# A new order for the first slots of a fused attention and MLP kernel, and a reordered end of batch 6

## Chip, cores and metric

The kernel runs on one core of a Trainium2 chip. The metric is the device time of one execution in microseconds (us); lower is better. TensorE (PE) does the matrix products, VectorE (DVE), ScalarE (ACT) and GpSimd (POOL) the elementwise work, and SyncE (SP) issues most DMAs.

## What is computed

```
def _attn_ref(x, state):                       # x: 8 batches, 8 heads, 512 x 64; state: 8, 8, 32 x 64
    a  = softmax(scale * x @ state.T);   xread = a  @ state
    a2 = softmax(scale * state @ x.T);   sread = a2 @ x
    return concatenate([xread, sread], axis=2)
def _moe_ref(x, w_in, w_out):                  # x: 4608 x 512 (heads side by side), w_in 512 x 2048
    h = x @ w_in
    g = h * tanh(softplus(h))
    return g @ w_out                           # w_out 2048 x 512
```

All of it is float32. The kernel splits every operand of a large product into a high part (a cast to a shorter float) and a low part (a subtraction), and adds three products: high by high, high by low, low by high. The weights arrive as 64-bit words and are made into floats on the chip: a scaling of the upper words (`hi`, `ho`; on DVE's help `ki`, `ko`), a rounding of the lower words (`ci`, `co` on ACT, `di`, `do` on DVE) and a join of both by DVE (`ji`, `jo`).

## The kernel before, in words

A batch goes through 16 chunks of the inner dimension of 2048, two to a slot, so eight slots. For the attention's read of x the kernel never forms xread: it multiplies the state's blocks with a slice of w_in once per slot (`sw_slice`, L576, tile `swp` in PSUM, cast to `swh` by ACT, low part `swl` by DVE), and then multiplies the softmax weights (`ah`, `al`, L469) with that (`gemm1`, L628, tile `ph`). ACT applies the activation (`mish`), a cast and a subtraction give `gh` and `gl`, and these are multiplied with w_out (`gemm2`, L700, tiles `acc`, for batch 0; `consume`, L1011, with seven products of sums, for later batches). The matrix `swp` comes from products on quarters of the PE array, which take few columns each.

**Order.** Nothing is ordered by a planner. Each of PE, DVE, ACT and POOL runs its instructions in exactly the order in which the program issues them (`InOrder`, L60). For batch 0 a long string of steps (L874 to L886) writes that order out by hand: each word names a step of the dictionary `steps` (L830), and a step that is a generator does one part at each mention. The names that matter: `sw0` (product, then ACT's cast, then DVE's low part of slice 0), `no` (softmax sums and normalizing), `pr0`, `pr1` (transpose on PE, `ah` by ACT, `al` by DVE of either half of the tokens), `fill` (matmuls on data at hand whose result is not used, two records for each), `qa`, `qb` (`first_quarter`, L761: slot 0's `gemm1` for one half of the tokens, for chunk a or b), `p1` to `p7` (slot n's `gemm1`), `ma0`, `mb0`, `m1` (activation and cast), `lg1` (low part of slot 1's `g`), `ja1`, `wha0`, `loa0`, `lo1` (join, high and low parts of a piece of w_out), `ga0`, `gb0` (slot 0's `gemm2` by tiles of 128 tokens, one chunk each), `g1` (the same for slot 1 with both chunks), `ldi`, `ldo` (DMA of a piece of w_in, of w_out). SP's DMAs wait in the order of their issue.

**Buffers.** PSUM has three pools: four banks `second_bank` (accumulators; at first also the transposes `at`), two `first_bank` (`ph`), and two `misc`. The raw w_in pieces 0, 1, 4, 5, 6 and 7 take turns in two buffers `raw`; pieces 2 and 3 lie where pieces 6 and 5 of w_out will be (`load_w_in`, L169). The place of piece 7 of w_out holds x of batch 0, then from step `X1` the turned x of batch 1.

**Later batches** have a table of one line per slot (L1081 to L1135), run by the loop at L1225: `G`, `M` are `gemm1` and activation of a chunk, `P` and `p` begin and end the preparation of a unit (casts, sums on POOL), `A` and `B` consume a unit on PE (some 2.5 us), `N0` is the next batch's first `sw_slice` (product, cast, low part), `SR` the state read (`sread`, L497), `TU` turns the exponentials and moves them by 16 DMAs (`e2_turned`, L391), `PR` is `ah` and `al` of the next batch. Batch 6's last line goes on with `rs`, `U`, `rt`, `W0`, `W1`: the eight batches' state reads are put together (`rt`: two transposes on PE and their high and low parts) and the state rows' own slots (`s_item`, L659) begin; they run as key "s" (L1144) before batch 7.

Of the kernel before, what the change touches and what calls it, by code (L numbers as in the profile page):

```python
# [17 lines left out]
P = 128  # L18
# [3 lines left out]
NC = H // 2  # L22
# [58 lines left out]
def state_attention_mish_kernel(ctx, tc, x, state, w_in, w_out, out):  # L81
# [87 lines left out]
    def load_w_in(e):  # L169


        shape, place = [P, NC, 2 * P, 2], {2: "wo6", 3: "wo5"}.get(e)
        if place:
            raw = const.tile(shape, U32, tag=place, name=f"wir_{e}")
        else:
            raw = pool.tile(shape, U32, tag="raw", name=f"wir_{e}", bufs=2)
        w = w_in.rearrange("(c p) f -> p c f", p=P)[..., 4 * e * P:4 * (e + 1) * P]
        for c in range(0, NC, 2):
            last["load"] = nc.sync.dma_start(
                raw[:, c:c + 2].rearrange("p c f w -> p c (f w)"), w[:, c:c + 2])  # L180
        return raw
# [93 lines left out]
    def attention(b, sn, x_in=None):  # L275
# [115 lines left out]
        def e2_turned():  # L391

            both = pool.tile([P, NC, 2, NT, NS], F32, tag="e2T", name=f"e2T_{b}", bufs=1)
            for kc in range(2):
                e2T[kc] = both[:, :, kc]
            u = pool.tile([P, 4, 2, NT * NS], F32, tag={0: "u0", 1: "wt"}.get(b, "sc"), name=f"u_{b}", bufs=1)
            for kc in range(2):
                dve.transpose(
                    u[:, :, kc].rearrange("i q (t n) -> i t q n", t=NT),
                    e2s[kc].rearrange("n (t q p) -> n t q p", t=NT, q=4))  # L400
            for c in range(NC):
                for q in range(4):
                    nc.sync.dma_start(
                        both[quad(q), c].rearrange("p k t n -> p (k t n)"), u[quad(c), q].rearrange("i k m -> i (k m)"))
# [92 lines left out]
        def sread(kc):  # L497

            if kc == 0:
                srd["bank"] = first_bank(f"srp_{b}")  # L500
            pr = srd["bank"][:, kc * D:(kc + 1) * D]
            for t in range(NT):
                for h4 in range(4):
                    o = slice(h4 * NS, (h4 + 1) * NS)
                    last["PE"] = pe.matmul(
                        pr[o],
                        e2T[kc][:, h4, t],
                        xss[b][:, h4, kc, t * D:(t + 1) * D],
                        start=(t == 0), stop=(t == NT - 1),
                    )  # L510
# [148 lines left out]
    def s_item(j, r, k):  # L659


        fc = 2 * r + k
        w = wis[B - 1, j][:, :, fc * P:(fc + 1) * P]
        if (j, r, k) == (0, 0, 1):
            both = pool.tile([P, 2, NC, P], F32R, tag="wt", name="w_0_0_1", bufs=1)
            hi, lo = both[:, 0], both[:, 1]
        else:
            hi, lo = (pool.tile([P, NC, P], F32R, tag="t", name=f"w{n}_{j}_{r}_{k}", bufs=5) for n in "hl")
        act.copy(hi, w)
        dve.tensor_sub(lo, w, as_f32(hi))  # L670
        yield
        ph = (misc, misc if (j, r) == (3, 1) else first_bank)[k](f"ph_s_{j}_{r}_{k}")
        for c in range(NC):
            pe.matmul(
                ph, hi[:, c], srT[c // 2][:, c % 2].rearrange("p i t -> p (i t)"), start=(c == 0), stop=(c == NC - 1))
        for c in range(NC):
            pe.matmul(
                ph[:, :256], lo[:, c], srT[c // 2][:, c % 2, 0], start=False, stop=(c == NC - 1), skip_group_check=True)
        yield
        unit = made["s", 0, 2 * j + r] if k else new_unit("s", 0, 2 * j + r)  # L680
        to = unit[:, 1 - k].rearrange("f h t -> f (h t)")
        act.copy(to, ph[:, 256:])
        dve.tensor_add(to, to, ph[:, :256])
        yield
        last["mish"] = act.activation(to, to, AF.Mish)
# [72 lines left out]
            phs[j] = [None, None]  # L758
        phs[j][k] = gemm1(0, j, aTs[0], sw, (k,))[0]

    def first_quarter(k, h):  # L761

        if 0 not in phs:
            phs[0] = [None, None]
        if phs[0][k] is None:
            phs[0][k] = first_bank(f"ph_0_0_{k}")
        of, to = slice(h * 256, (h + 1) * 256), phs[0][k].rearrange("f (t q p) -> f t q p", t=NT, q=4)[:, :, 2 * h:2 * h + 2]
        swh, swl = (t[:, :, k * P:(k + 1) * P] for t in sw[0])
        products = [(w[:, kc], aTs[0][kc][n][:, of].rearrange("n (q t p) -> n t q p", q=2, t=NT)) for w, n in ((swh, 0), (swh, 1), (swl, 0)) for kc in range(2)]
        for i, (w, a) in enumerate(products):  # L770
            pe.matmul(to, w, a, start=(i == 0), stop=(i == 5))
# [48 lines left out]
    def load_x_in(b):  # L820
# [51 lines left out]
    }  # L872
    begun = {}
    for step in """  # L874
            st st st x0 x1 ldi0 x2 x3 sc hia0 ldi1 acc sc sc sc hib0 sc dia0 tr0 tr0 tr1 tr0 ldo0 tr1 jia0 cib0
            tr1 st ex0 ex1 jib0 no fill6 sw0 cib1 cia1 no coa0 ldi2 sw0 fill2 ldo1 pr0 pr0 hia1 ldi4 pr1 ldi3
            dob0 pr0 hib1 pr1 sw0 hoa0 qa0 qb0 ldo2 ldi5 jia1 jib1 di2 hob0 hi2 fill2 pr1 sw1 sw1 qb1 qa1 ji2
            ldo3 fill2 sw1 ma0 joa0 mb0 job0 ko1 ma0 mb0 wha0 sw2 p1 lx co1 loa0 sw2 la0 ci3 m1 ldo4 whb0 ga0
            lb0 sw2 lob0 ko1 ldo5 ga0 ga0 ja1 ga0 gb0 hi3 ho2 m1 ji3 gb0 gb0 lg1 ja1 gb0 p2 ci4 co2 ldo6 ldi6
            lo1 do3 sw3 g1 jo2 sw3 hi4 ji4 jo2 sw3 lo2 n2 g1 n2 X1 ho3 lg2 ldi7 g1 X2 jo3 p3 mm1 hi5 ho4 m3 sw4  # L880
            di5 g1 X3 sw4 jo3 g2 ji5 co4 sw4 g2 m3 ho5 lo3 jo4 lg3 ST X0 g2 jo4 g2 co5 sw5 p4 sw5 n4 sw5 hi6 di6
            lo4 n4 XD0 ja5 ci7 g3 g3 ja5 g3 lg4 p5 ji6 hi7 m5 g3 g4 mm0 g4 lo5 ji7 sx6 SC m5 g4
            sx6 lg5 SC sx6 SC ee0 xi2 ldo7 ee1 TR1 g4 ho6 ee0 p6 ho7 co6 ee1 TR0 g5 TR1 g5 TR0 EX1 tu EX0 ja6 n6 g5
            n6 NO xz0 ja6 co7 g5 NO xy0 next lg6 loa6 lob6 PR0 p7 PR1 g6 g6 n7 PR0 PR1 ja7 PR0 next g6 PR1 n7
            g6 next ja7 lg7 lo7
# [125 lines left out]
    def consume():  # L1011
# [61 lines left out]
    def half_slot(key, j, at):  # L1073
# [4 lines left out]
        elif ready and (ready[0][:2] != (key, 0) or ready[0][2] < j + (j == SLOTS - 1 and at)):  # L1078
# [183 lines left out]
```

## Time and profile before

| what | us |
|---|---|
| median of 3 runs | 625.49 (624.79 to 626.25) |
| the profiled execution, its own time | 624.49 |
| its span, first to last instruction | 622.6 |
| PE busy in the span | 615.7 |
| DVE, ACT, POOL busy | 448.1, 368.2, 232.8 |

The span is 1.9 us shorter than the profiled execution's own time. A row of a timeline has the start, the time taken, the engine, line, operation, tiles written and read, shape and count of merged instructions. Matmuls overlap: a row of n matmuls takes n spacings and the tail of the last, so lengths of PE work are taken from the start of one row to the start of another.

### The profile page before, as it was taken

How to read it: one execution, taken by the hardware profiler on the slowest of the kernel's cores; microseconds unless marked ns; L12 is line 12 of the kernel's file. 1: busy time of each engine (PE TensorE's matmuls, PEld its weight loads, DVE VectorE, ACT ScalarE, POOL GpSimd, SP SyncE). 2: the span in 40 equal slices, each digit the busy share in tenths (PEclk: the TensorE clock that was granted, in tenths of full speed). 3: DMA queues.
4: the chain of work that ended last, by engine and by line, in shares of the span. 5: the costliest groups of instructions: out<-in, count | busy, mean ns of one | idle time of the engine just before them, and what ended most of it. 6: DMA issues, size and time to landing. Idle time of an engine off the chain costs nothing.

```text
span 622.6 us, 13825 instructions
## 1 busy us (share of the span) xinstructions
PE 615.7 (99%) x5388; PEld 534.2 (86%) x5388; DVE 448.1 (72%) x763; ACT 368.2 (59%) x762; POOL 232.8 (37%) x348
## 2 busy tenths in 40 slices
PE   8999999999999999999999999999999999999997
PEld 6777777788888898888988898889889999898997
DVE  5999976667778885969577764869386887535364
ACT  5999876466457454666446545655455766544442
POOL 0000000235375164226622573246522744443284
PEclk9999999999999999999999999999999999999999
DMA  8995922944552164524554274415355332321011
GB/s 324 413 357 156 366 64 76 308 147 123 133 182 70 36 174 123 172 93 127 144 169 137 78 193 137 165 39 162 111 172 166 106 118 87 103 68 26 10 35 35
DMA packets 71970, 88.79 MB, mean 143 GB/s; under 512 B 13793, under 2 KB 49121, under 8 KB 71905
## 3 DMA queue, kind: packets, MB, share of 16 engines
q1 hardware_dynamic: 71472, 87.71, 44.8%
q8 instruction: 43, 0.70, 0.5%
q10 hardware_dynamic: 432, 0.20, 0.1%
q14 instruction: 23, 0.18, 0.1%
HBM read 62.85 MB, written 13.11 MB: 122 GB/s over the span
## 4 chain that ended last, share of the span: by engine, by line
PE 98%; DMA 1%; DVE 1%; ACT 0%; issue 0%
PE ph L73 29%; PE acc_top L73 15%; PE acc_one L73 11%; PE acc_two L73 11%; PE acc_end L73 9%; PE acc L73 8%; PE swp L73 5%; PE ph_s L73 4%; PE srp L73 1%; PE sc L73 1%; PE acc_s_one L73 1%; PE acc_s_top L73 1%; PE acc_s_two L73 1%; DMA sn<-in_state_dram 1%; PE acc_s_end L73 0%; PE scT L73 0%
## 5 line engine op out<-in xcount | busy, mean ns | idle before, releaser
L73 POOL TENSOR_TENSOR sums<-u 128x256 f32<-128x256 f32 x96 | 77.9, 812 | 192.3 <-DVE gl L73 117.1
L73 ACT ACTIVATE u<-ph 128x256 f32<-128x256 f32 x224 | 73.5, 382 | 80.0 <-PE ph L73 78.6
L73 DVE TENSOR_TENSOR gl<-u,gh 128x384 fp32r<-128x384 f32 (+1 forms) x112 | 70.3, 627 | 69.3 <-ACT gh L73 60.8
L73 POOL TENSOR_TENSOR sums<-sums,u 128x128 f32<-128x128 f32 x192 | 113.4, 591 | 15.1
L73 DVE TENSOR_TENSOR gl<-sums,gh 128x512 fp32r<-128x512 f32 x96 | 78.8, 821 | 31.0 <-ACT gh L73 30.9
L73 ACT CAST gh<-u 128x384 fp32r<-128x384 f32 (+1 forms) x112 | 59.2, 529 | 67.5 <-PE acc_end L73 49.8
L73 PE MATMUL acc_top<-wo,gh 128*128 128x256 f32 (+1 forms) x448 | 93.5, 300 | 0.0
L73 POOL TENSOR_TENSOR w_sums<-w_sums 128x256 f32<-128x256 f32 x28 | 25.3, 902 | 151.1 <-ACT gh L73 109.7
L73 ACT CAST gh<-sums 128x512 fp32r<-128x512 f32 x96 | 59.6, 620 | 29.5 <-POOL sums L73 29.4
L73 PEld LDWEIGHTS acc_top<-wo,gh 128*128 128x128 f32 x448 | 71.2, 191 | 4.5 <-issue 1.6
L73 PE MATMUL ph<-ah,swh 128*128 128x512 f32 (+1 forms) x228 | 70.5, 391 | 0.0
L73 PE MATMUL ph<-al,swh 128*128 128x512 f32 (+1 forms) x228 | 69.9, 388 | 0.2 <-DVE al L73 0.2
L73 PE MATMUL ph<-ah,swl 128*128 128x512 f32 (+1 forms) x228 | 69.9, 388 | 0.0
L73 PE MATMUL acc_top<-wo,gl 128*128 128x256 f32 (+1 forms) x224 | 66.9, 298 | 0.0
L73 PEld LDWEIGHTS ph<-al,swh 128*128 128x128 f32 x228 | 42.5, 188 | 10.0 <-DVE al L73 0.4
L73 PEld LDWEIGHTS ph<-ah,swl 128*128 128x128 f32 x228 | 42.6, 188 | 9.3
L73 DVE TENSOR_TENSOR swl<-swp,swh 128x512 fp32r<-128x512 f32 (+1 forms) x60 | 36.3, 644 | 18.5 <-ACT swh L73 18.5
L73 PEld LDWEIGHTS ph<-ah,swh 128*128 128x128 f32 x228 | 39.5, 188 | 8.3 <-issue 0.8
L73 PEld LDWEIGHTS acc_top<-wo,gl 128*128 128x128 f32 x224 | 42.7, 191 | 1.3
L73 ACT CAST swh<-swp 128x512 fp32r<-128x512 f32 (+1 forms) x60 | 30.6, 565 | 16.5 <-PE swp L73 16.5
L73 PE MATMUL acc<-wo,gh 128*128 128x512 f32 x128 | 40.0, 394 | 0.0
L73 PE MATMUL acc_one<-wo,gh 128*128 128x256 f32 x192 | 39.8, 289 | 0.0
(233 smaller groups left out, 1393.0 us busy)
## 6 DMA issues: line engine op xcount, KB each, us to landing
w_in<-w_in_again SPq DMA_DIRECT2D x27, 1024.0 KB, 6.0
x<-in_x_dram SPq DMA_DIRECT2D x32, 256.0 KB, 4.3
wir<-in_moe_w_in_dram SPq DMA_DIRECT2D x16, 512.0 KB, 9.1
wor<-in_moe_w_out_dram SPq DMA_DIRECT2D x16, 512.0 KB, 8.5
x_rows<-x_turned SPq DMA_DIRECT2D x56, 128.0 KB, 2.4
out_dram<-sums SPq DMA_DIRECT2D x25, 256.0 KB, 4.4
x_in<-in_x_dram SPq DMA_DIRECT2D x24, 256.0 KB, 4.8
w_in_again<-w_in_sb SPq DMA_DIRECT2D x4, 1024.0 KB, 7.4
```

What stands on the lines that cost most here:

```text
L73: made = method(*args, **kwargs)
```

## The change

Batch 0: a new string of steps. Slot 0's `gemm1` becomes one step `q` for both chunks of a half of the tokens, with its results in two of the four accumulator banks in place of the two `ph` banks. Piece 4 of w_in is loaded into the place of piece 7 of w_out. There are two `fill2` in place of `fill6` and three `fill2`. `sw2` stands behind six of slot 0's eight `gemm2` tiles, not ahead of `p1`; `ci4` on ACT becomes `di4` on DVE, and `di2` on DVE becomes `ci2` on ACT; `ji3` moves behind `lo1`, `X3` behind `ST`.

Batch 6's end: `SR` comes directly behind the unit `A`, and `N0`'s product behind the unit `B`, ahead of the transposes `rt`; its cast stands behind `W1`, and its low part at item 4 of the state rows' slots. `N0` uses the `first_bank` pair and the state read of batch 7 a `misc` bank, and so the first three pairs of the state rows' items both use `misc`. For batch 7, four of the 16 DMAs of `TU` are issued by ACT in slot 6. In unit 7 of batch 6's first half the fifth product comes second.

```diff
-        shape, place = [P, NC, 2 * P, 2], {2: "wo6", 3: "wo5"}.get(e)
+        shape, place = [P, NC, 2 * P, 2], {2: "wo6", 3: "wo5", 4: "wo7"}.get(e)
...
+            if b < B - 1:
+                move(nc.sync, *range(4))
+            else:
+                move(nc.sync, *range(3))
+                yield
+                move(act, 3)
+            yield
...
-                srd["bank"] = first_bank(f"srp_{b}")
+                srd["bank"] = (misc if b == B - 1 else first_bank)(f"srp_{b}")
...
-        ph = (misc, misc if (j, r) == (3, 1) else first_bank)[k](f"ph_s_{j}_{r}_{k}")
+        ph = (misc, misc if (j, r) in ((0, 0), (0, 1), (1, 0), (3, 1)) else first_bank)[k](f"ph_s_{j}_{r}_{k}")
...
-    def first_quarter(k, h):
+    def first_quarters(h):
         if 0 not in phs:
+            phs[0] = [second_bank(f"ph_0_0_{k}") for k in range(2)]
+        of = slice(h * 256, (h + 1) * 256)
+        products = [
+            (k, w[:, kc, k * P:(k + 1) * P], aTs[0][kc][n][:, of].rearrange("n (q t p) -> n t q p", q=2, t=NT))
+            for w, n in ((sw[0][0], 0), (sw[0][0], 1), (sw[0][1], 0)) for k in range(2) for kc in range(2)]
+        for i, (k, w, a) in enumerate(products):
+            to = phs[0][k].rearrange("f (t q p) -> f t q p", t=NT, q=4)[:, :, 2 * h:2 * h + 2]
+            pe.matmul(to, w, a, start=(i in (0, 2)), stop=(i in (9, 11)))
...
     for step in """
-            st st st x0 x1 ldi0 x2 x3 sc hia0 ldi1 acc sc sc sc hib0 sc dia0 tr0 tr0 tr1 tr0 ldo0 tr1 jia0 cib0
-            tr1 st ex0 ex1 jib0 no fill6 sw0 cib1 cia1 no coa0 ldi2 sw0 fill2 ldo1 pr0 pr0 hia1 ldi4 pr1 ldi3
-            dob0 pr0 hib1 pr1 sw0 hoa0 qa0 qb0 ldo2 ldi5 jia1 jib1 di2 hob0 hi2 fill2 pr1 sw1 sw1 qb1 qa1 ji2
-            ldo3 fill2 sw1 ma0 joa0 mb0 job0 ko1 ma0 mb0 wha0 sw2 p1 lx co1 loa0 sw2 la0 ci3 m1 ldo4 whb0 ga0
-            lb0 sw2 lob0 ko1 ldo5 ga0 ga0 ja1 ga0 gb0 hi3 ho2 m1 ji3 gb0 gb0 lg1 ja1 gb0 p2 ci4 co2 ldo6 ldi6
-            lo1 do3 sw3 g1 jo2 sw3 hi4 ji4 jo2 sw3 lo2 n2 g1 n2 X1 ho3 lg2 ldi7 g1 X2 jo3 p3 mm1 hi5 ho4 m3 sw4
-            di5 g1 X3 sw4 jo3 g2 ji5 co4 sw4 g2 m3 ho5 lo3 jo4 lg3 ST X0 g2 jo4 g2 co5 sw5 p4 ...
+            st st st x0 x1 ldi0 x2 x3 sc hia0 ldi1 acc sc sc sc hib0 sc dia0 tr0 tr0 tr1 tr0 ldo0 tr1 jia0
+            cib0 tr1 st ex0 ex1 jib0 sw0 no fill2 cia1 cib1 hia1 ldi2 sw0 no fill2 ldo1 pr0 hib1 pr0 ldi4 pr1
+            coa0 ldi3 jia1 pr0 pr1 sw0 hoa0 q0 ldo2 jib1 ldi5 hob0 hi2 pr1 sw1 sw1 q1 dob0 joa0 ldo3 sw1 job0
+            ma0 wha0 mb0 ma0 loa0 ko1 p1 lx la0 mb0 whb0 co1 ci2 m1 ldo4 ga0 lb0 lob0 ji2 ko1 ldo5 ga0 ga0 ja1
+            ga0 gb0 gb0 sw2 hi3 sw2 m1 gb0 sw2 gb0 ja1 lg1 ci3 p2 lo1 ho2 co2 ldo6 ldi6 ji3 do3 g1 sw3 hi4 jo2
+            di4 sw3 ji4 jo2 sw3 lo2 n2 g1 n2 X1 ho3 lg2 ldi7 g1 X2 jo3 p3 mm1 hi5 ho4 m3 sw4 di5 g1 sw4 jo3 g2
+            ji5 co4 sw4 g2 m3 ho5 lo3 jo4 lg3 ST X3 X0 g2 jo4 g2 co5 sw5 p4 ...
...
+        if unit == (B - 2, 0, SLOTS - 1):
+            steps.insert(1, steps.pop(4))
...
         B - 2: """
...
-            P G0 M0 p G1 M1 P p NO PR0 PR1 A P p B
-            P G0 M0 p G1 M1 N0 PR0 PR1 P p N0 N0 A P p SR0 SR1 SR0 SR1 w3 rs B U rt W0 A W1 P p""",
+            P G0 M0 p G1 M1 P TU p NO PR0 PR1 A P p B
+            P G0 M0 p G1 M1 P p A SR0 SR1 SR0 SR1 P p w3 B rs N0 U rt W0 A W1 N0 P p PR0 PR1""",
...
+                if i == 4:
+                    next(begun[B - 2, "N0"], None)
...
-            return sw_slice(key + 1, i, bank=misc if i or key == B - 2 else first_bank, w=wis[key + 1, i // 2])
+            return sw_slice(key + 1, i, bank=misc if i else first_bank, w=wis[key + 1, i // 2])
```

## Rows read from the trace of the kernel before

**Rows 1.** The page, part 1: an engine's busy us, share of the span, instructions.

```profile
PE 615.7 (99%) x5388; PEld 534.2 (86%) x5388; DVE 448.1 (72%) x763; ACT 368.2 (59%) x762; POOL 232.8 (37%) x348
```

**Rows 2.** Busy time by stretch: us, PE, PEld, DVE, ACT, POOL, granted clock, DMA share, GB/s.

```profile
10.00:20.00 10.00, 9.26 (x82) 6.29 (x80) 9.68 (x21) 8.75 (x17) 0.00 (x0) 1.00 1.04 409
```

**Rows 3.** Timeline of PE, 0 to 40 us: start, us, what, count.

```profile
1.36 2.50 PE L73 MATMUL warm<-ident 128*128 128x128 f32 x10 [1.36 <-POOL ident masks.py:199]
...
12.68 1.50 PE L73 MATMUL acc<-xT 128*128 128x128 f32 x12
...
16.53 0.50 PE L73 MATMUL ph<-ah,swh 128*128 128x256 f32 x2
...
19.39 0.66 PE L73 MATMUL swp<-w_in_sb,bd 64*32 64x256 f32 x16
...
22.15 0.79 PE L73 MATMUL swp<-w_in_sb,bd 64*32 64x256 f32 x16
22.87 1.21 PE L73 MATMUL ph<-ah,swh 128*128 128x512 f32 x4
...
25.78 0.63 PE L73 MATMUL acc<-wo,gh 128*128 128x512 f32 x2
...
34.15 0.66 PE L73 MATMUL swp<-w_in_sb,bd 64*32 64x256 f32 x16
34.74 0.72 PE L73 MATMUL acc<-wo,gh 128*128 128x512 f32 x2
...
38.97 0.63 PE L73 MATMUL ph<-ah,sw 128*128 128x512 f32 x2
```

**Rows 4.** Timeline of ACT, 12 to 39 us.

```profile
12.88 0.60 ACT L73 ACTIVATE e<-scT 128x512 f32<-128x512 f32 x1 [0.26 <-PE scT L73]
...
15.05 0.66 ACT L73 CAST swh<-swp 128x256 fp32r<-128x256 f32 x2
15.89 0.59 ACT L73 CAST ah<-at 128x512 fp32r<-128x512 f32 x1 [0.18 <-PE at L73]
16.37 1.23 ACT L73 ACTIVATE wir<-wir 128x512 f32<-128x512 f32 x2
...
19.11 1.20 ACT L73 ACTIVATE wir<-wir 128x1024 f32<-128x1024 f32 x1
...
20.84 1.28 ACT L73 ACT_TABLE_LOAD   x1
```

**Rows 5.** Timeline of DVE, 12 to 39 us.

```profile
16.51 0.69 DVE L73 TENSOR_TENSOR al<-at,ah 128x512 fp32r<-128x512 f32 x1 [0.20 <-ACT ah L73]
17.11 0.74 DVE L73 TENSOR_TENSOR swl<-swp,swh 128x256 fp32r<-128x256 f32 x2
17.78 1.28 DVE L73 SCALAR_TENSOR_TENSOR w_in_sb<-wir 128x512 uint32<-128x512 uint32 x2
...
23.34 0.78 DVE L73 CAST gh<-g 128x512 fp32r<-128x512 f32 x2
...
33.16 1.22 DVE L73 TENSOR_TENSOR wo<-w,wo 128x1024 fp32r<-128x1024 f32 x1
```

**Rows 6.** Timeline of PE, batch 6's end: inside a unit; state rows' item 3.

```profile
490.90 0.28 PE L73 MATMUL acc_one<-wx_w_in,gl 128*128 128x256 f32 x1
491.11 0.47 PE L73 MATMUL acc_two<-wx_w_in,gh 128*128 128x256 f32 x2
...
499.67 1.09 PE L73 MATMUL ph_s<-srT,wh 128*128 128x512 f32 x4
```

**Rows 7.** Timeline of DVE, batch 6's end; state rows' item 1.

```profile
486.58 1.27 DVE L73 TENSOR_TENSOR swl<-swp,swh 128x512 fp32r<-128x512 f32 x2
...
490.55 0.42 DVE L73 SCALAR_TENSOR_TENSOR sums<-sums,acc_two 128x256 f32<-128x256 f32 x1
...
498.74 0.41 DVE L73 TENSOR_TENSOR u_s<-u_s,ph_s 128x256 f32<-128x256 f32 x1
```

**Rows 8.** Timeline of SP, 471 to 483 us: the 16 DMAs of step `TU`.

```profile
471.60 11.20 SPq L403 DMA_DIRECT2D e2T<-u  x16
```

More of the change, by code (lines that the diff above doesn't have):

```diff
@@ L400, in e2_turned, with move @@
                     e2s[kc].rearrange("n (t q p) -> n t q p", t=NT, q=4))
[L401 to L404, printed above, removed]
+            def move(by, *qs):
+                for c in range(NC):
+                    for q in qs:
+                        by.dma_start(
+                            both[quad(q), c].rearrange("p k t n -> p (k t n)"), u[quad(c), q].rearrange("i k m -> i (k m)"))
+            if b < B - 1:
[5 more added lines that the diff above has]
+            yield
         two = range(2)
@@ L759, in first_half @@
         phs[j][k] = gemm1(0, j, aTs[0], sw, (k,))[0]
-    def first_quarter(k, h):
+    def first_quarters(h):
         if 0 not in phs:
[L764 to L771, printed above, removed]
+            phs[0] = [second_bank(f"ph_0_0_{k}") for k in range(2)]
[6 more added lines that the diff above has]
+            pe.matmul(to, w, a, start=(i in (0, 2)), stop=(i in (9, 11)))
     def mish_half(j, k, copy=None):
@@ L848, in state_attention_mish_kernel @@
         "goa": lambda o: round_low(rawo[o][:, a1], by_pool=True), "gob": lambda o: round_low(rawo[o][:, b1], by_pool=True),
-        "qa": lambda h: first_quarter(0, h), "qb": lambda h: first_quarter(1, h),
+        "q": first_quarters,
         "nexf": lambda _: sw_slice(1, 0, bank=first_bank), "sx": lambda j: sw_slice(0, j),
@@ L874, in state_attention_mish_kernel @@
     for step in """
-            st st st x0 x1 ldi0 x2 x3 sc hia0 ldi1 acc sc sc sc hib0 sc dia0 tr0 tr0 tr1 tr0 ldo0 tr1 jia0 cib0
-            tr1 st ex0 ex1 jib0 no fill6 sw0 cib1 cia1 no coa0 ldi2 sw0 fill2 ldo1 pr0 pr0 hia1 ldi4 pr1 ldi3
-            dob0 pr0 hib1 pr1 sw0 hoa0 qa0 qb0 ldo2 ldi5 jia1 jib1 di2 hob0 hi2 fill2 pr1 sw1 sw1 qb1 qa1 ji2
-            ldo3 fill2 sw1 ma0 joa0 mb0 job0 ko1 ma0 mb0 wha0 sw2 p1 lx co1 loa0 sw2 la0 ci3 m1 ldo4 whb0 ga0
-            lb0 sw2 lob0 ko1 ldo5 ga0 ga0 ja1 ga0 gb0 hi3 ho2 m1 ji3 gb0 gb0 lg1 ja1 gb0 p2 ci4 co2 ldo6 ldi6
-            lo1 do3 sw3 g1 jo2 sw3 hi4 ji4 jo2 sw3 lo2 n2 g1 n2 X1 ho3 lg2 ldi7 g1 X2 jo3 p3 mm1 hi5 ho4 m3 sw4
[L881 to L885, printed above, removed]
+            st st st x0 x1 ldi0 x2 x3 sc hia0 ldi1 acc sc sc sc hib0 sc dia0 tr0 tr0 tr1 tr0 ldo0 tr1 jia0
[4 more added lines that the diff above has]
+            di4 sw3 ji4 jo2 sw3 lo2 n2 g1 n2 X1 ho3 lg2 ldi7 g1 X2 jo3 p3 mm1 hi5 ho4 m3 sw4 di5 g1 sw4 jo3 g2
+            ji5 co4 sw4 g2 m3 ho5 lo3 jo4 lg3 ST X3 X0 g2 jo4 g2 co5 sw5 p4 sw5 n4 sw5 hi6 di6 lo4 n4 XD0 ja5
+            ci7 g3 g3 ja5 g3 lg4 p5 ji6 hi7 m5 g3 g4 mm0 g4 lo5 ji7 sx6 SC m5 g4 sx6 lg5 SC sx6 SC ee0 xi2
+            ldo7 ee1 TR1 g4 ho6 ee0 p6 ho7 co6 ee1 TR0 g5 TR1 g5 TR0 EX1 tu EX0 ja6 n6 g5 n6 NO xz0 ja6 co7 g5
+            NO xy0 next lg6 loa6 lob6 PR0 p7 PR1 g6 g6 n7 PR0 PR1 ja7 PR0 next g6 PR1 n7 g6 next ja7 lg7 lo7
             """.split():
```

## The prediction, made before the changed kernel was run

> **What bounds the kernel now.** I read the page first: PE is busy for 615.7 of the span's 622.6 us [rows 1]. So time can be saved in three ways only: less PE work, less waiting in the first microseconds, or less at the very end. Then the busy times by stretch: from 10 to 20 us DVE has 9.68 of 10 us, ACT 8.75 and the DMA engines a share of 1.04 [rows 2]. That stage is full everywhere; in it a reordering moves waits as easily as it removes them. Then the PE timeline of that stage [rows 3], with ACT's and DVE's beside it [rows 4, 5]: PE looks busy because fills stand in its waits. The old string has twelve of them, 24 records, one about every 0.112 us (12 in 1.50 us, the last with a tail of 0.27) [rows 3]. From p1 on, at 22.87, I see no wait in PE's rows: whatever is won before that is kept if ACT, DVE and DMA keep up.
>
> **Batch 0, step by step.** Successive ops on DVE or ACT start some 0.1 us before the last one's end: two of ACT's half pieces take 1.23 us [rows 4], so one more in a queue costs 0.56.
>
> Eight of the twelve fills go: 16 records x 0.112 = 1.8 us of PE work. That is the most this part can give; how much it gives hangs on what PE then waits for.
>
> *sw0 earlier, fill6 gone.* sw0's two misc banks are held until the second exponential has read its scores, at 13.48 (12.88 + 0.60 [rows 4]), so its products still run at about 13.6. Nothing on the path changes: DVE's normalizing sets the time of the transposes as before.
>
> *q0.* ACT now has one more half piece (hib1) between sw0's casts (from 15.05) and ah0. Two casts in 0.56, hib1 0.56, ah0 0.59 [rows 4]: ah0 ends at 16.75, not 16.48, a loss of 0.25. DVE's al0 follows (0.69 [rows 5]) to 17.45, swl0 (0.74) to 18.1. The second chunk's bank can be had only when al0 has read the transposes' bank, at the same 17.45. So PE starts q0 at 16.8, stands until 17.5, and has ten products of 0.116 left, the last of them behind swl0: it ends at about 18.6. Before, q0 ran from 16.53 to 18.85 (sw1 at 19.39 less a fill2 of 0.54 [rows 3]), since it did all six products of a chunk before the other chunk's. Gain 0.25.
>
> *sw1, q1.* Before, sw1 stood behind that fill2. Now it needs jib1 alone, which follows swl0 on DVE since jia1 has moved ahead of al0: half of 1.28 [rows 5], so 18.7. sw1 at 18.8, q1 0.6 later (as 34.15 to 34.74 [rows 3]) at 19.4. al1 follows jib1 at once, to 19.3, with di2 gone; no wait is left in q1, and it takes 12 x 0.116 + 0.1 = 1.5: it ends at 20.9. Before: 22.15 less a fill2, 21.6. Gain so far 0.7.
>
> *p1.* Before, fill2 and sw2 (22.15 to 22.87, 0.72 [rows 3]) stood ahead of it, and its two ph banks had to wait for slot 0's activation. Both are gone: slot 0's results lie elsewhere. swh1: hoa0 and hob0 behind ah1, then hi2 (1.20 [rows 4]) bring ACT to 19.9, the casts to 20.5, in time. p1 starts at 20.9 against 22.87: 1.95 earlier. Slot 0's gemm2 follows at 23.7. Its last operand, la0: casts at 20.5, table load 1.28 [rows 4], activation 0.6, so DVE casts gh at 22.45 (0.35), then two subtractions of 0.6 and 0.7: 24.1, wanted by the third product at 24.15.
>
> *sw2 comes back* behind six tiles, for 0.6 and 0.2 of changes in the use of the array: 0.8. At p2 the gain is then 1.15: p2 at 20.9 + 2.8 (p1) + 5.5 (eight tiles; six take the 4.2 from 34.74 to 38.97) + 0.8 = 30.0 [rows 3].
>
> *lo1.* DVE from the first cast of gh to the end of lo1 does the same work as before (23.34 to 34.38 [rows 5]) less one cast (0.35, put ahead), with ji2 for ji3. It starts 0.9 earlier, so it ends 1.2 earlier at best, at 33.2; a wait for ci2 on ACT may add 0.1. The first g1 tile starts at 32.8 and wants lo1 by its second product, 33.05. A wait of 0.15 to 0.3; I take 0.25.
>
> Then sw3, two tiles and p3: p3 at 38.05 against 38.97 [rows 3]; there swl3 and the activation that frees p3's banks come within some 0.1 us of their need. Gain kept: **0.9 us**. Bounds: 1.8 (every removed fill, no new wait) and, if DVE's chain slips further at q0, lo1 or swl3 (another 0.3 to 0.5 each), about 0.
>
> *Costed at nothing*: piece 4's new place lets its DMA be issued earlier, but the transfers run at a share of 1.04 [rows 2] in the same order, so pieces land when they did. ci2 for di2 and di4 for ci4 swap 1.2 us of ACT against 0.7 of DVE, included above. X3 behind ST gives DVE 0.6 us for lo3 and lg3; if that cover goes, g3 waits for lg3 by some tenths.
>
> **Batch 6's end.** PE's work is the same; only its order changes. Before, acc_two's first product starts 0.21 us after the row ahead of it, where the products of this width stand 0.12 apart, and the one after it follows after 0.19 (0.47 less a tail of 0.28) [rows 6]: PE waits until DVE's last reading of the old bank has ended, 490.55 + 0.42 = 490.97 [rows 7]. That DVE chain stands behind swl (1.27) [rows 7], which now moves to item 4 of the state rows. So this wait, 0.17, goes, and a change between N0's small products and a unit becomes one between N0 and the transposes, worth up to 0.1. SR now has 1.2 us less for the moved exponentials: 16 DMAs in 11.2 us on SP [rows 8], 0.7 each; without four of them the last is issued 2.8 us earlier. On ACT the four issues fall ahead of a cast whose unit is consumed a slot later. N0's casts and PR's (two each, 0.59 by ah's row [rows 4]) now stand ahead of the state rows' first evacuation on ACT, which may be late by 0.8. With two misc banks for the first six items, item 3 takes item 1's bank: DVE read it by 499.15 [rows 7], PE wanted item 3 at 499.67 [rows 6], so 0.5 is to spare. Between +0.5 (a late evacuation, beyond that cover) and -0.3; I take **-0.2**, since the wait seen is the nearest row.
>
> **Sum**: -0.9 - 0.2 = -1.1 us, so 623.4 for an execution like the profiled one (624.49), which lies 1.0 below the median of the runs. From that median, 625.49, it is **624.4**. A measurement of this kernel can tell some 0.2%, 1.25 us, from no change; the forecast is just inside it.
>
> **Rivals.**
> 1. *The waits come back.* DVE at 9.68 of 10 [rows 2] is the true bound of the first 40 us, and la0, lo1 and swl3 each come a few tenths later than I have them. For: three arrivals within 0.1 us of their need. Against: from 23 to 34 us DVE itself starts 0.9 earlier. Gain 0 to 0.6: 624.9 to 625.5, or a little above if the state rows wait too. Chance 0.24.
> 2. *All fills pay.* The bank for q0's second chunk is free earlier and lo1 is in time: 1.8 at most, and 0.3 at the end: 623.4 to 624.0. Against: g1's second product asks for lo1 before DVE can have it. Chance 0.20.
> 3. *The clock falls: slower.* The warm-up's matmuls are more than 0.2 us apart (10 in 2.50) where the fills of the same shape are 0.112 apart [rows 3]: PE can run at half its clock. Fills now end near 15, and up to q0 at 16.8 PE has 0.9 us of transposes and waits. If the clock drops to 1.2 GHz there and rises with p1, the transposes (0.9), q0 (1.4), half of sw1 (0.3) and q1 (1.4) take twice as long: 4.0 us more, of which some 1.3 falls into waits that stand there anyway. 2.7 - 1.1 = +1.6: 627.1. It decides from the point at which the granted clock of 13 to 21 us is under 1.00. Against: 10 to 20 us has 1.00 now [rows 2], with much the same transposes and waits ahead of q0. Chance 0.06.
>    The Trainium skill, "TensorE: Matmul & The Clock Gate", Part 4, says that transposes do not count as activity like other matmuls, which speaks for this rival. No run here shows it yet: before, two fills more stood in that stretch, and the clock stayed.
>
> The remaining 0.50 is the forecast, a gain of 0.7 to 1.5.
>
> **Numbers.** Of the forecast's 0.50, 0.19 lies beyond 1.25 us; with rival 2 that gives 0.39 for faster. Rival 3 and a tail from batch 6's end give 0.07 for slower; 0.54 is left for same. The forecast's own range is 624.0 to 624.8; down through rival 2 and up through rival 1 it is 623.3 to 625.8.
>
> **What would show it.** p1 near 20.9, p2 near 30.0, p3 near 38.0; a late second product in the first g1 tile; granted clock 1.00; swp directly ahead of srTp, and acc_two 0.12 behind its predecessor; PE busy less by some 1.5 us. I am wrong if p3 starts later than 38.6 or earlier than 37.6, or if the state rows' items show waits of PE.

## The result, and the profile after

The changed kernel is slower: 629.33 us (median of six runs, 627.43 to 630.72) against 625.12 us beside it (six runs), a ratio of 1.0063 with a 95% interval of 1.0047 to 1.0080. Two more sets of runs gave 1.0029 (1.0018 to 1.0040) and 1.0051 (1.0031 to 1.0071). So it loses between 1.4 and 4.2 us; 624.4 had been forecast. The profiled execution took 627.51 us, 3.0 us more than the 624.49 of before; its span is 625.7.

The page, part 1, and the busy times from 10 to 20 us (columns as in [rows 1, 2]):

```profile
PE 616.3 (99%) x5372; PEld 531.9 (85%) x5372; DVE 449.0 (72%) x763; ACT 368.5 (59%) x762; POOL 231.8 (37%) x348
...
10.00:20.00 10.00, 8.94 (x73) 5.28 (x72) 9.67 (x21) 8.77 (x17) 0.00 (x0) 1.00 1.04 410
```

PE has 16 records less, the eight fills, and yet counts as busy for 0.6 us longer than in [rows 1]: a wait inside a row of products is counted as busy, as in the first tile of slot 1's `gemm2` at 33.05 in this trace, where a pair that takes 0.62 elsewhere takes 0.86. The granted clock of this stretch is 1.00.

Timeline of PE, start to slot 4's sw (start, us, what, count, idle time before it and who ended it); these answer to [rows 3]. The last fence is slot 4's sw before:

```profile
16.90 0.51 PE L73 MATMUL ph<-ah,swh 128*128 128x256 f32 x2
...
19.02 0.66 PE L73 MATMUL swp<-w_in_sb,bd 64*32 64x256 f32 x16
19.61 0.74 PE L73 MATMUL ph<-ah,swh 128*128 128x256 f32 x4
...
21.14 1.10 PE L73 MATMUL ph<-ah,swh 128*128 128x512 f32 x4
...
30.24 0.63 PE L73 MATMUL ph<-ah,sw 128*128 128x512 f32 x2
...
38.21 0.67 PE L73 MATMUL ph<-ah,sw 128*128 128x512 f32 x2
...
39.54 1.30 PE L73 MATMUL ph<-ah,sw 128*128 128x512 f32 x4 [0.19 <-DVE sw L73]
...
41.70 0.66 PE L73 MATMUL swp<-w_in_sb,bd 64*32 64x256 f32 x16
```

```profile
41.86 0.66 PE L73 MATMUL swp<-w_in_sb,bd 64*32 64x256 f32 x16
```

The start comes within 0.25 us of the forecast at every step, p3 with a gain of 0.76 (38.21 against 38.97). Traces differ by some tenths ahead of the stretch that was edited: the row `scT<-mx,ident` starts at 10.95 here and at 10.86 before, and between 10.57 and 11.52 in the other runs' traces. Then 0.6 of the gain goes: p3's third group of products waits for swl3, and slot 4's sw stands at 41.70 against 41.86 before, a gain of 0.16.

The large loss comes at 78 us. SP's DMA issues around 60 to 68 us, first of before, then of after:

```profile
60.58 0.61 SPq L1172 DMA_DIRECT2D w_in_again<-w_in_sb  x1
61.30 3.26 SPq L136 DMA_DIRECT2D x_in<-in_x_dram  x4
64.61 1.03 SPq L191 DMA_DIRECT2D wor<-in_moe_w_out_dram  x2
65.74 2.13 SPq L136 DMA_DIRECT2D x_again<-in_x_dram  x4
68.19 0.56 SPq L1172 DMA_DIRECT2D w_in_again<-w_in_sb  x1
```

```profile
61.15 1.28 SPq L1185 DMA_DIRECT2D w_in_again<-w_in_sb  x2
62.55 4.63 SPq L136 DMA_DIRECT2D x_in<-in_x_dram  x4
67.22 1.11 SPq L191 DMA_DIRECT2D wor<-in_moe_w_out_dram  x2
```

The write of `w_in_again`'s second quarter (1 MB, the copy of `w_in` that later batches read back) has moved ahead of batch 2's `x_in` and of `wor_7`, the last piece of w_out. Its own issue takes 0.7 us, the four of `x_in` behind it 4.63 instead of 3.26; `wor_7` is issued at 67.22 instead of 64.61, and its second half lands at 74.56 instead of 71.35. Who waits for that, on ACT, first before and then after:

```profile
71.53 2.16 ACT L73 ACTIVATE wor<-wor 128x1024 f32<-128x1024 f32 x2 [0.79 <-DMA wor<-in_moe_w_out_dram]
```

```profile
74.66 2.17 ACT L73 ACTIVATE wor<-wor 128x1024 f32<-128x1024 f32 x2 [4.08 <-DMA wor<-in_moe_w_out_dram]
...
79.19 1.09 ACT L73 ACTIVATE g<-ph 128x512 f32<-128x512 f32 x2
```

Behind that wait stands slot 6's activation, which frees the banks of p7. PE before, then after:

```profile
78.30 0.74 PE L73 MATMUL ph<-ah,sw 128*128 128x512 f32 x2
```

```profile
79.84 0.73 PE L73 MATMUL ph<-ah,sw 128*128 128x512 f32 x2 [1.65 <-ACT g L73]
```

p7 is 1.54 late. The first tile of g6 then waits for its operand (82.75, 1.03 us where such a pair takes 0.62), and from there on the kernel is 2.0 us behind. At 228 to 233 us another 1.2 goes: DVE waits for `x_in` and then PE for DVE:

```profile
225.72 0.71 DVE L73 STREAM_TRANSPOSE x_turned<-x_in 128x512 f32<-128x512 f32 x1 [2.05 <-DMA x_in<-in_x_dram]
```

```profile
231.32 0.39 PE L73 MATMUL acc_one<-wx_w_in,gl 128*128 128x256 f32 x1 [0.53 <-DVE gl L73]
```

Batch 6's end, PE, for [rows 6]:

```profile
492.14 1.09 PE L73 MATMUL swp<-w_in,bd 64*32 64x256 f32 x32
493.17 0.44 PE L73 MATMUL srTp<-ident,srds 128*128 128x128 f32 x2
...
494.03 0.28 PE L73 MATMUL acc_one<-wx_w_in,gl 128*128 128x256 f32 x1
494.16 0.48 PE L73 MATMUL acc_two<-wx_w_in,gh 128*128 128x256 f32 x2
```

swp stands directly ahead of srTp and acc_two 0.13 behind its predecessor instead of 0.21; the kernel is 3.2 us late ahead of this stretch and 3.1 us late after it. In four of the six runs the mean granted clock was 0.996 or 0.997, and those took 629.3 to 630.7 us; this trace is one of the two others, so it explains 3.0 us and not the rest.

### The profile page after: what moved, and what is told of

It is laid out like the page before. It is cut to its first block, busy times and chain, and to the rows that moved or that the text cites. A ratio compares the mean times of both kernels' runs of the same rounds, so it can differ in the third digit from the quotient of the medians.

```text
span 625.7 us, 13795 instructions
## 1 busy us (share of the span) xinstructions
PE 616.3 (99%) x5372; PEld 531.9 (85%) x5372; DVE 449.0 (72%) x763; ACT 368.5 (59%) x762; POOL 231.8 (37%) x348
## 4 chain that ended last, share of the span: by engine, by line
PE 84%; DMA 1%; DVE 0%; issue 0%; SPq 0%; ACT 0%; DVEq 0%
PE ph L73 24%; PE acc_top L73 14%; PE acc_one L73 11%; PE acc_two L73 11%; PE acc_end L73 9%; PE swp L73 4%; PE ph_s L73 4%; PE acc L73 2%; PE srp L73 1%; DMA out_dram<-sums 1%; PE acc_s_one L73 1%; PE acc_s_top L73 1%; PE acc_s_two L73 1%; PE sc L73 1%; PE acc_s_end L73 0%
```

## The experiments

| kernel | us (runs) | before beside it | ratio, 95% interval |
|---|---|---|---|
| changed, wor_7's load first | 624.87 (11) | 624.74 | 0.9998 to 1.0016 |
| before, second write early | 626.25 (7) | 624.74 | 1.0015 to 1.0037 |
| changed first slots alone | 626.99 (5) | 624.74 | 1.0027 to 1.0052 |
| batch 6's end alone | 624.47 (11) | 624.74 | 0.9986 to 1.0004 |
| changed, again | 626.04 (7) | 624.66 | 1.0018 to 1.0040 |
| wor_7 first, swl3 ahead of the join | 624.55 (11) | 624.66 | 0.9992 to 1.0010 |
| the same, SP padded | 624.68 (11) | 624.66 | 0.9995 to 1.0015 |
| first slots alone, wor_7 first | 624.64 (11) | 624.66 | 0.9992 to 1.0010 |
| wor_7 first, swl3 ahead, PE padded | 623.70 (12) | 624.55 | 0.9983 to 1.0000 |
| changed, PE padded | 627.65 (5) | 624.55 | 1.0038 to 1.0062 |
| changed, third time | 627.24 (6) | 624.55 | 1.0031 to 1.0071 |
| before, eight fills less | 625.57 (11) | 624.65 | 1.0005 to 1.0023 |

**The order of two transfers put back.**

```diff
+            if (k, i) == ("o", 7):
+                last["o7"] = last["load"]
...
-                    with behind("move"):
+                    with behind("move", *(("o7",) if g == 1 else ())):
```

> The changed kernel, with one thing put back: the write of w_in_again's second quarter is issued behind the load of wor_7, as in the kernel before (the first quarter's write stays ahead). Theory A (the order of two transfers: wor_7 landed at 74.56 us instead of 71.35 because 1 MB of w_in_again went ahead of it): ScalarE's 4.08 us wait for wor_7 shrinks to under 1 us, p7 starts at 77.5 to 78.4 us instead of 79.84, and the 2 us that stood in the trace at 88 us are gone: 625.0 to 626.3 us, the upper end if the 1.2 us lost at 228 to 233 us have another cause. Theory B (the clock: the first slots as they are now listed cost the clock in most executions, wherever wor_7 lands): the trace gains its 2 us, but the median of the runs stays at 627.0 us or more with mean granted clocks of 0.997 in most of them.

The write is issued behind `wor_7`, and ACT's wait is 1.35 us:

```profile
65.26 0.99 SPq L191 DMA_DIRECT2D wor<-in_moe_w_out_dram  x2
66.29 0.56 SPq L1187 DMA_DIRECT2D w_in_again<-w_in_sb  x1
```

```profile
72.26 2.18 ACT L73 ACTIVATE wor<-wor 128x1024 f32<-128x1024 f32 x2 [1.35 <-DMA wor<-in_moe_w_out_dram]
```

```profile
78.44 0.74 PE L73 MATMUL ph<-ah,sw 128*128 128x512 f32 x2
```

p7 runs without a wait, 0.04 us past what theory A gave; ACT's wait is longer than its "under 1 us", and the time, 624.87, is just under its range. No run had a clock under 0.999. Theory A holds, theory B falls: the same first slots keep the clock. Over all the runs here a mean clock under 0.999 was seen in 7 of 29 executions of kernels with the changed first slots and the early write, and in none of 56 with `wor_7`'s load first.

**The reverse: before, with both quarters written early.**

```diff
+    def write_w_in(_):
+        for g in range(2):
+            with behind("move"):
+                last["load"] = nc.sync.dma_start(w_in_again[:, :, g * G:(g + 1) * G], w_in_sb[:, :, g * G:(g + 1) * G])
...
-            sx6 lg5 SC sx6 SC ee0 xi2 ldo7 ee1 ...
+            sx6 lg5 SC sx6 SC ee0 wy xi2 ldo7 ee1 ...
...
-                for g in range(2 * n, 2 * n + 2):
+                for g in range(2 * n, 2 * n + 2) if n else ():
```

> The kernel before, with both quarters of w_in_again written ahead of x_in and wor_7, the order that the changed kernel has; nothing else is changed. Theory A: wor_7 lands some 3 us later, ScalarE waits about 4 us for it, p7 starts 1.5 to 2.5 us later and the kernel takes 626.8 to 629.5 us, the upper end if the clock falls in some executions as it did in the changed kernel. Theory B (the first slots as relisted are what costs): at most 1 us is lost, 625.0 to 626.2 us, and no execution shows a clock of 0.997.

1.5 us slower. In its trace p7 starts at 80.04 (before 78.30):

```profile
80.04 0.73 PE L73 MATMUL ph<-ah,sw 128*128 128x512 f32 x2 [1.85 <-ACT g L73]
```

The first tile of g6 adds 0.4, so 2.2 stand in the trace and 1.5 in the median. The median, 626.25, lies between the two ranges: theory A's began at 626.8 and was too high, theory B's ended at 626.2; the late p7 is what A gave and B did not. The price of the order alone, in the kernel before, is 1.5 to 2.2 us; nothing of it comes from the first slots.

**Each part alone.** The first slots without batch 6's end, and batch 6's end without the first slots:

> The changed kernel without its second part: batch 6's end is that of the kernel before, the first slots are the changed ones. If batch 6's end is worth 0.1 us, as the two traces have it, 629.4 us, the same as the changed kernel (628.6 to 630.2). A rival, that the falls of the clock come from batch 6's end: 627.5 us or less, all clocks at 0.999 or 1.000.

> The kernel before with the second part of the change alone: batch 6's end (state read between the units, next state product in the turn, its cast later, and the four transfers of e2T for the last batch on ScalarE's queue). As the two traces have it, 0.1 us less than before: 624.6 to 625.4 us. The rival, that the clock falls come from here: 626.5 us or more, with clocks of 0.997.

The first slots alone cost 2.3 us, not the 4.2 of the first runs, with every clock at 1.000. That is what the rival expected, the falls of the clock coming from batch 6's end; but batch 6's end alone is 0.3 lower than before, a little under its range and by its interval not to be told from nothing, and its clocks are 0.999 and 1.000 too. Whether the falls belong to the kernel at all was now open.

**The changed kernel twice more.**

> The changed kernel as it is, once more, because four of its first six executions had a mean granted clock of 0.996 to 0.997 and took 629.3 to 630.7 us, and two had 0.999 and 1.000 and took 627.5. The trace explains 627.5 (2.0 us by wor_7's late landing, 1.2 us at 228 to 233 us, less what the first slots win). Theory A (the late wor_7 starves TensorE and with that the clock falls now and then): the executions again fall in two groups, near 627.4 with clocks of 0.999 or 1.000 and near 629.5 with 0.997, the median between. Theory B (the second group came from the conditions of those runs and is no part of the kernel): all executions at 626.9 to 627.9 us.

> The changed kernel as it is, beside the two others and on the same chip, and once more for its spread: its first runs had a median of 629.33 us with clocks down to 0.996, the second 626.04 with none under 0.999. If the clock's falls belong to the kernel wherever it runs, some executions here show 0.997 and 629 us; if they came with the first chip, all stand at 625.5 to 627.5 us.

The second set, batch 6's end included, had no clock under 0.999 and took 625.49 to 627.16, in the median lower than theory B gave and not in the two groups of theory A. The third set had one run of six at 0.997, and that one took 630.29 where the others took 626.27 to 628.18. PE's wait ahead of p7 was 1.03 us in the one profile and 1.29 in the other. The falls come with this kernel, but not in each execution; that they don't come from batch 6's end is shown by the one fall that a profile caught, at 80 us (below).

**swl3 ahead of the join.**

```diff
-            di4 sw3 ji4 jo2 sw3 lo2 ...
+            di4 sw3 sw3 ji4 jo2 lo2 ...
```

> The changed kernel with w_in_again's second quarter written behind wor_7's load, and with VectorE's two casts of sw's third slice (swl3) listed ahead of the join of w_in's fourth piece instead of behind it. In the trace of the kernel without this second edit VectorE stood 0.51 us ahead of that join, swl3 ended at 40.12 us and p3, begun at 38.49, waited for it; slot 4's sw stood at +0.15 against before where p3 had stood at -0.48. If that wait is what ate the first slots' gain: swl3 ends near 38.0, p3 runs without a wait, the gain of 0.6 us stays: 624.1 to 624.5 us. If the next engine is as late (the join, then the cast and the low part of w_out's second piece): 624.7 to 625.1, no change.

DVE around the join of piece 4, first in the changed kernel, then in before, then with this edit:

```profile
27.33 1.22 DVE L73 SCALAR_TENSOR_TENSOR wor<-wor 128x1024 f32<-128x1024 f32 x1
28.58 1.23 DVE L73 SCALAR_TENSOR_TENSOR w<-wor 128x1024 uint32<-128x1024 uint32 x1
...
36.13 0.69 DVE L73 TENSOR_SCALAR wir<-wir 128x1024 uint32<-128x1024 uint32 x1
37.32 1.23 DVE L73 SCALAR_TENSOR_TENSOR w_in_sb<-wir 128x1024 uint32<-128x1024 uint32 x1 [0.50 <-DVE wir L73]
```

```profile
36.62 1.23 DVE L73 SCALAR_TENSOR_TENSOR w_in_sb<-wir 128x1024 uint32<-128x1024 uint32 x1 [0.50 <-ACT wir L73]
```

```profile
35.88 0.69 DVE L73 TENSOR_SCALAR wir<-wir 128x1024 uint32<-128x1024 uint32 x1
36.48 0.75 DVE L73 TENSOR_TENSOR sw<-swp,sw 128x256 fp32r<-128x256 f32 x2
37.14 1.22 DVE L73 SCALAR_TENSOR_TENSOR w_in_sb<-wir 128x1024 uint32<-128x1024 uint32 x1
```

In the changed kernel DVE stood 0.50 us between the rounding of piece 4 (`di4`) and its join (`ji4`); now swl3 fills that gap, and p3 has no wait. Before, the same join had a gap of 0.50 too, but there it waited for ACT's scaling of the upper words, which ended at 36.60; in the changed kernel that ended at 35.33. What makes the join wait 0.50 us for DVE's own rounding stays open: reading what the instruction directly ahead wrote is not enough, since the join of a w_out piece at 28.58, in the same trace, started 0.03 us behind the scaling of its tile. The trace keeps 0.80 at 115 us. The median, 624.55, is nevertheless that of before, just above the expected range: half a microsecond is lost again at 228 us, and 0.3 at 233.

**A wrong guess at that loss: SP's code.**

```diff
-                        nc.sync.dma_start(w_in_again[:, :, g * G:(g + 1) * G], w_in_sb[:, :, g * G:(g + 1) * G])
+                        for c in range(NC) if g else (slice(0, NC),):
+                            nc.sync.dma_start(w_in_again[:, c, g * G:(g + 1) * G], w_in_sb[:, c, g * G:(g + 1) * G])
```

> As the kernel with swl3 ahead of the join, and three of w_in_again's four writes are issued in four transfers of 256 KB each instead of one of 1 MB, so that SyncE issues nine transfers more before batch 3's e2T. In the traces a 16 KB load on the instruction queue stands at each of SyncE's long issues, some 15 transfers apart; in the kernels with the changed first slots one falls at 208.7 to 210.6 us, into e2T's sixteen transfers (the third to fifth land 0.5 to 1.6 us late), in the kernel before at 204.2 and 219.0, outside. If that place costs the 0.4 us lost at 228 to 233 us: no e2T of that batch lands over 2.0 us after its issue, acc_two near 229 us and acc_one near 233 us stand as they stood at 115 us against before, 0.3 to 0.4 us less than the kernel without the padding. The rival, that the loss there has another cause: the same time, with the e2T landings even.

The load on queue q8 stands at 208.4, 0.4 us later than without the padding, and still falls into e2T's third to fifth transfer, which land 2.7 to 3.4 us after their issue, though SP had issued nine transfers more by then; the time is the same. So these loads aren't SP's code, and the theory falls as stated.

**PE's code.** The page of before counts 43 loads of 16 KB on q8 and 5388 matmul and 5388 weight-load records, 251 records for each load (the 10971 below also count 195 waits of PE); after has 42 and 5372. The eight fills that went are 16 matmul and 16 weight-load records. The test puts 32 instructions back where PE waits:

```diff
+        def pad(n, pt):
+            for _ in range(n):
+                last["PE"] = pe.matmul(
+                    pt[:32, :32], xTs[NC - 1][:32, :32], xTs[NC - 1][:32, :32], start=True, stop=True)
...
-            ... sc dia0 tr0 tr0 tr1 tr0 ldo0 ...
+            ... sc dia0 pad4 tr0 tr0 tr1 pad4 tr0 ldo0 ...
```

> The kernel with wor_7's load first and swl3 ahead of the join, and eight matmuls of 32x32 that nobody reads are added at the start, in TensorE's two waits at 8.9 to 9.3 and 10.4 to 10.7 us. The theory: the 16 KB loads on instruction queue q8 are TensorE's code (43 of them for 10971 recorded matmuls and weight loads, one for each 255), so each stands at a fixed place of TensorE's program. The changed first slots issue 16 matmuls and their 16 weight loads less than before (fills left out), so every later load comes some 32 instructions later in the work: at 208.0 and 220.8 us, amid batch 3's e2T and x_in transfers, not at 204.2 and 219.0. Padding SyncE's queue with nine transfers left it in place. With 32 TensorE instructions put back the loads stand at 203 to 204.5 and at 217.5 to 219 us again, no e2T of that batch lands over 2.0 us after its issue, and the 0.5 to 0.8 us lost at 226 to 235 us are back: 623.7 to 624.2 us. If the loads are not TensorE's, or are not what costs there: 624.4 to 624.9 us, with e2T's third to fifth transfer late again.

> The changed kernel with the same eight matmuls of 32x32 in TensorE's waits at the start, and nothing else. If the place of TensorE's code loads costs 0.6 to 1.2 us at 226 to 235 us and the order of the two transfers 1.1 to 2 us at 77 to 88, the first of the two goes and the second stays: 0.6 to 1.2 us less than the changed kernel on the same chip, p7 still late by 1 to 1.7 us. The rival: no change beside the changed kernel.

The first of these two, with `wor_7` first, swl3 ahead and the padding, takes 623.70 us, 0.85 less than before beside it; without the padding it had taken 624.55, and had been level with before. The loads come at 203.5 and 218.5, DVE's waits are those of before (rows below), and nothing is lost between 210 and 244 us. The reverse of it, the kernel before with eight fills less and every other queue as it was:

```diff
-            tr1 st ex0 ex1 jib0 no fill6 sw0 cib1 ...
-            dob0 pr0 hib1 pr1 sw0 hoa0 qa0 qb0 ldo2 ldi5 jia1 jib1 di2 hob0 hi2 fill2 pr1 sw1 ...
+            tr1 st ex0 ex1 jib0 no sw0 cib1 ...
+            dob0 pr0 hib1 pr1 sw0 hoa0 qa0 qb0 ldo2 ldi5 jia1 jib1 di2 hob0 hi2 pr1 sw1 ...
```

> The kernel before with eight of its twelve fills left out (the six ahead of sw's first slice and the two ahead of its second), nothing else: the queues of the other engines keep their order. TensorE issues 32 instructions less, as in the changed kernel. The theory of the code loads: q8's loads come later in the work, at 207 to 208.5 and 220 to 222 us, e2T's third to fifth transfer land 2.4 to 3.7 us after their issue, and 0.4 to 1.0 us is lost at 226 to 235 us, whatever the start wins (0 to 0.6 us): 624.3 to 625.4 us, with the trace 0.4 us or more worse against before at 235 us than at 115 us. The rival: the loads stay at 204 and 219 and nothing is lost there. The rival of the prediction, that TensorE's clock falls at the start for want of these fills: the granted clock is 0.5 for some us from 12 to 20 us and the kernel takes 626.5 us or more.

0.92 us slower, from taking eight fills out; 625.57 is just above the expected range. DMA queues from 207 to 211 us (q8's load and e2T's issues with the median from issue to landing), before, where no q8 load stands in this window, and then with the fills out:

```profile
e2T<-u SPq DMA_DIRECT2D x7, 32.0 KB, 1.9
```

```profile
q8 instruction: 1, 0.02, 1.5%
...
e2T<-u SPq DMA_DIRECT2D x6, 32.0 KB, 2.1
```

DVE from 221 to 229, before, with the fills out, and with the fills' number put back by padding (the 623.70 kernel):

```profile
222.50 1.46 DVE L73 STREAM_TRANSPOSE x_turned<-x_in 128x512 f32<-128x512 f32 x2 [0.34 <-DMA x_in<-in_x_dram]
224.71 1.22 DVE L73 TENSOR_TENSOR w_sums<-wo 128x1024 f32<-128x1024 f32 x1 [0.75 <-DMA out_dram<-sums]
```

```profile
223.46 0.71 DVE L73 STREAM_TRANSPOSE x_turned<-x_in 128x512 f32<-128x512 f32 x1 [1.42 <-DMA x_in<-in_x_dram]
...
227.22 1.23 DVE L73 TENSOR_TENSOR w_sums<-wo 128x1024 f32<-128x1024 f32 x1 [2.02 <-DMA out_dram<-sums]
```

```profile
222.00 1.38 DVE L73 STREAM_TRANSPOSE x_turned<-x_in 128x512 f32<-128x512 f32 x2 [0.33 <-DMA x_in<-in_x_dram]
224.14 1.22 DVE L73 TENSOR_TENSOR w_sums<-wo 128x1024 f32<-128x1024 f32 x1 [0.77 <-DMA out_dram<-sums]
```

With the fills out, q8's loads stand at 209.0 and 224.0 (before 204.2 and 219.0; in its trace only 42 PE records start between 204.2 and 208.7, so there 32 instructions are some 4 us). Three of e2T's transfers land 2.4 to 3.1 us after their issue where 1.85 is usual, SP issues behind them later, the last two of `x_in` and the stores that free w_sums' buffer land later, and PE waits for gl:

```profile
230.11 0.39 PE L73 MATMUL acc_one<-wx_w_in,gl 128*128 128x256 f32 x1 [0.52 <-DVE gl L73]
```

Against before this trace stands at +0.30 at 115 us and at +1.98 at 233. It started late by 0.30 ahead of the edited stretch (11.16 against 10.86), and stands at +0.25 at 21.6 us, so ahead of slot 1 the fills' removal won next to nothing. The 10 to 20 us stretch has a granted clock of 1.00 without those fills.

All 14 traces agree on the place, measured from the swp that starts at 210.14 before to the one at 243.59. In five of them the load stands ahead of batch 3's e2T (before, batch 6's end alone, before with the early write, and the two padded on PE), and those four lose 0.00 us there against before. In the other nine the load stands amid e2T, and they lose 0.43 to 1.64 us.

The padding alone, on the changed kernel, moved the loads too (208.3 and 222.2 in a kernel 3.8 us late there, and e2T lands evenly), and its trace loses nothing from 210 to 244 us, where the changed kernel's three traces lose 0.6 to 1.2. But the time rose by 0.4 (627.65 against 627.24, within their spreads), where 0.6 to 1.2 less was expected: its trace loses 4.0 us at p7, where the three others lose 1.5 to 2.1. The profile happened to catch a fall of the clock. Busy times by stretch (columns as in [rows 2]), and PE:

```profile
78.00:80.00 2.00, 0.17 (x8) 0.00 (x0) 1.97 (x4) 1.97 (x4) 0.00 (x0) 1.00 0.82 281
80.00:82.00 2.00, 1.38 (x3) 1.16 (x4) 1.97 (x6) 1.97 (x3) 0.00 (x0) 0.62 0.18 51
82.00:84.00 2.00, 2.00 (x6) 1.55 (x5) 1.89 (x4) 2.00 (x3) 0.00 (x0) 0.53 0.18 51
84.00:86.00 2.00, 2.00 (x10) 1.60 (x10) 2.00 (x4) 1.44 (x4) 0.00 (x0) 1.00 0.21 57
```

```profile
80.62 1.22 PE L73 MATMUL ph<-ah,sw 128*128 128x512 f32 x2 [2.45 <-ACT g L73]
...
84.99 0.62 PE L73 MATMUL acc<-wo,gh 128*128 128x512 f32 x2
```

In this execution `wor_7` was later still (it lands at 75.39) and PE stood 2.45 us ahead of p7. The granted clock is 0.5, the level of 1.2 GHz, from 80.46, late in that wait, to 83.87. p7 and what follows it to g6's first tile take 4.37 us (80.62 to 84.99) instead of 2.90 (78.30 to 81.20 before): 1.5 us on top of the wait. A fall as long as this one makes a mean clock of 0.997 over 626 us, which is what three of the four slowest of the first six executions had; that theirs fell at the same place is likely and not shown, since none of them was profiled.

**The first slots alone with the order put back.**

> The changed first slots alone (batch 6's end as before), with w_in_again's second quarter written behind wor_7's load. If the two parts add up, it stands above the kernel with both parts (624.9 us) by what batch 6's end alone won, 0.3 us: 625.0 to 625.3 us. If batch 6's end is worth nothing behind the changed first slots, 624.7 to 624.9 us.

624.64 against 624.87 with both parts, each the same as the before beside it: no difference, the lower of the two cases; what batch 6's end is worth behind the changed first slots can't be told from zero.

## Why the prediction was wrong

**The first slots: right in mechanism and size, up to p3.** q0 at 16.90 (forecast 16.8), sw1 19.02 (18.8), q1 19.61 (19.4), p1 21.14 (20.9), p2 30.24 (30.0), lo1's wait in g1's first tile (0.86 for a pair that takes 0.62, so 0.24; forecast 0.25), p3 38.21 (38.05). The gain there is 0.76 against 0.9. (At p2 the sum names a gain of 1.15, but its own 30.0 is 1.26 ahead of the 31.26 of before; measured it was 1.02.)

**What p3 had no room for.** The prediction had swl3 "within some 0.1 us" of its need. It was 0.6 late: the join of piece 4 stood 0.50 us behind the rounding of its tile on DVE, and swl3 stood behind both. Its own sum ("di4 for ci4 swap 1.2 us of ACT against 0.7 of DVE, included above") counted busy times and no gap. This is rival 1 for one of its three arrivals; putting swl3 ahead of the join took the wait away.

**The step that failed.** This is "the transfers run at a share of 1.04 [rows 2] in the same order, so pieces land when they did", a term that the prediction put at nothing. Up to 34 us the pieces did come in the same order, some 0.6 us later than before; at 61 us the order did not hold, where the prediction no longer looked. "Nothing is ordered by a planner" holds for the four engines that `InOrder` ties to the program's order; a DMA on SP's queue is held only behind the marks that `behind` names. So the 1 MB write, whose line comes later in the program than `wor_7`'s load, now goes first, `wor_7` lands 3.2 us later and p7 starts 1.5 us later. Putting the order back took 2.3 us off the first slots alone (626.99 to 624.64, in two sets of runs) and making it in the kernel before cost 1.5. What in the new list made that write come first stays open. The prediction's own signs of being wrong, p3's place and waits in the state rows' items, both stayed clear, since neither looks at 40 to 490 us.

**What was costed at nothing and had no line at all.** The fills' removal was counted as PE time won. But PE's instructions come by DMA too, 16 KB at a time, and 32 instructions less move the later loads against the kernel's transfers. The load that stood ahead of batch 3's e2T now falls into it: 0.92 us in the kernel before. "Whatever is won before that is kept if ACT, DVE and DMA keep up" named the condition, and the DMA half of it failed twice. In the old list the fills were not what PE stood behind: without eight of them it had won next to nothing at 21.6 us.

**Rival 3: wrong place.** The clock does fall in some executions, and makes them slower, but not at 13 to 21 us: that stretch has 1.00 in every trace here, also without the fills. The Trainium skill, "TensorE: Matmul & The Clock Gate", Part 4, says that transposes don't count as activity like other matmuls; no run here shows a fall from it. Its section "Why this matters for your kernels" names idle gaps between bursts of matmuls as what drops the clock. The fall at 80.46, late in a wait of 2.45 us, agrees in kind, though this one gap is shorter than those that the section warns of. Waits of 1.03 to 1.65 at the same place, in four other profiles of kernels with the changed first slots, and of 1.85 in before with the early write, came without a fall.

**Batch 6's end.** Forecast -0.2; -0.1 in the trace and -0.3 in the runs of it alone, where the interval holds zero. Half the wait ahead of acc_two went (0.21 to 0.13 behind its predecessor, of 0.17 forecast). "If the state rows' items show waits of PE" didn't come about.

With the three costs taken away (order, swl3, code loads) the kernel gains 0.85 us, where 1.1 had been forecast; that version, 623.70 us, has the lowest median of all measured here, at a ratio of 0.9992 whose interval just reaches 1, so a gain is likely and not certain.

## What to carry to other kernels

After a change in a hand-listed order, compare the order of transfers on every DMA queue for the whole kernel, not only where the list was edited: one 1 MB write ahead of the last weight cost 1.5 to 2.3 us, where the edit was to win 1.1. Removing instructions from an engine with a long program moves its code loads against all later transfers, so a loss far from the edit, with the same instruction order on every engine, is looked for in the instruction queues. Watch the granted clock where a change makes PE wait longer: here waits of 1.03 to 1.85 us left it at 1.00, and one of 2.45 us came with a fall that cost 1.5 us more.

## What the runs showed of the hardware that was not expected

- q8 carries 16 KB of PE's code for each 251 recorded PE instructions, through the whole execution. Eight dummy matmuls of 32x32 moved those loads from 208.0 and 220.8 us to 203.5 and 218.5; nine transfers more on SP's queue moved them by 0.4 and 0.7.
- A code load that meets small transfers delays more than itself: in the nine traces where one met batch 3's e2T, three of the sixteen transfers took 2.4 to 3.7 us to land instead of 1.85, SP's issue of the fifth took 1.1 to 1.7 us instead of 0.59, and PE lost 0.43 to 1.64 us by 244 us; in the five others it lost nothing.
- On DVE the join of piece 4 started 0.50 us after the end of the rounding that wrote its tile, directly ahead of it, and with swl3 between them there was no gap; other instructions that read what the one directly ahead wrote started 0.03 us behind it (28.58 in the changed kernel's trace). What tells the two cases apart was not found.
